# A list scheduler's due times taken backwards from TensorE's list, fewer and larger opening transfers, and spare matrix products in TensorE's idle stretches

## The chip, the cores and the metric

The kernel runs on one core of a Trainium2 chip. The metric is the device time of one execution in microseconds (us). The engines are TensorE (PE, with its weight loads as PEld), VectorE (DVE), ScalarE (ACT), GpSimd (POOL) and SyncE (SP), whose queue issues nearly all the transfers.

## The reference

Two operations, one on the other's result. First a light convolution: for each of 33280 tokens (8 batches of 4160) and each of 8 heads, a softmax over 7 taps weighs the last 7 tokens. Then a layer with a maximum of three projections:

```python
w = np.exp(weight_gen - weight_gen.max(-1, keepdims=True))
w = w / (w.sum(-1, keepdims=True) + 1e-09)
x_unf = x_pad[:, idx, :].reshape(B, S, K, H, group)      # 7 taps of 192 features
out = np.einsum('bshk,bskhg->bshg', w, x_unf).reshape(B * S, D)
h = np.maximum(np.maximum(out @ w1, out @ w2), out @ w3)  # 192 -> 768
return (h @ w_out).astype(np.float32)                     # 768 -> 192
```

x and weight_gen are float32; the four weight matrices are float64.

## The kernel before

**Tiles and stages.** Each of the 128 partitions holds 260 consecutive tokens. They are worked off in 65 chunks of four tokens per partition (512 tokens). `load_super` loads the first chunk alone and then two chunks at a time: `wt` (the tap weights) and `xt` (the tokens, and ahead of them six of the tokens before). The first two loads miss those six in the tile of a partition's predecessor, so halo rows are copied from the neighbouring partition's end: one transfer for each batch (line 305), in the first load half of them on ACT's queue. `softmax` has seven steps: maximum (DVE), subtraction (POOL), exponential (ACT), sum (DVE), addition of 1e-9 (DVE, line 344, tile `den`), reciprocal (DVE), product (POOL).

`taps` makes a chunk's convolution: for each of four tokens a product over seven taps on POOL (`r`, line 370) and its sum on DVE (`acc`, line 382). `blocks` turns the chunk so that features lie on partitions: for chunks 0 and 1 on TensorE (lines 402 and 403), for all later ones with one 32x32 block transpose on DVE (`room`, line 421) and 24 small copies on ACT (line 432). `parts` splits the result into high and low parts for fp32r products: `xa_hi`, `xa_lo`, `xb`, `xc`.

**Products.** All products of the main part stand at line 802, in `products`. Each bank (an accumulator of 128 x 512) is computed in two halves of 64 rows of the array, lower (list L) and upper (list U); between the lower half's last product and the upper half's first stands a nop in SP's queue (line 808). `up` makes for each of six j two banks of nine products, for w2 - w1 and w3 - w1; then ReLU on ACT (`m`, line 859), the maximum on DVE (line 867), and the split into `h_hi` (ACT, line 871) and `h_lo` (DVE or POOL, line 878). `down` makes for each of four tokens 18 products of each half, with w_out and with the composed matrix w1 @ w_out (`wca`, `wcb`), and adds on DVE (line 935). The order on TensorE is written out by hand: the twelve up-groups of a chunk, in whose middle (`DOWN_AT`) stand the four down-groups of the chunk before it.

**The opening.** The weights come as float64 and are converted by bit operations in `single`: one step on ACT (line 573) and four on DVE (lines 579 to 604), for nine tiles of the upper 128 rows (`prepare_a`, whose products are `wa_hi` and, on POOL, `wa_lo`, line 643), three tiles of the lower 64 rows (`prepare_b`: `wb_hi`, `wb_lo`) and three of w_out (`prepare_down`). After chunk 0's up-groups TensorE turns w1 (`turn_weights`, lines 731 and 733) and after half of chunk 1's it composes w1 @ w_out (`compose`, line 750; `wca` and `wcb`, lines 759 and 767).

**The order of the work.** Every operation is a task with an engine, a cost, the tasks it depends on, the buffers it holds and a due time. `Plan.order` simulates the engines: whenever one is free, it starts among its ready tasks whose buffers are to be had the one with the smallest due time. TensorE's lists L and U alone are worked off in their written order. The order of starts in this simulation is the order of the program on each engine. Due times come from fixed offsets to `needed(c)`, 22 + 21 c us, in most places, and from a running clock behind the products:

```python
    def needed(c):
        return FIRST + PERIOD * c
...
            p = plan.add(
                "POOL", 2.75, product, [ready[s], *loads[s][1]], due - 26 + 3 * t, [hr, hx, hw]
            )
```

Of the kernel before, what the change touches and what calls it, by code (L numbers as in the profile page):

```python
# [20 lines left out]
class Hold:  # L21


    def __init__(self, pool):
        self.pool, self.users, self.taken, self.tile = pool, 0, False, None


class Task:
    def __init__(self, engine, cost, emit, deps, due, holds, end):
        self.engine, self.cost, self.emit, self.due = engine, cost, emit, due  # L30
        self.holds, self.after = holds, []
        self.end = cost if end is None else end
        self.missing = 0
        for d in deps:
            d.after.append(self)
            self.missing += 1
        for h in holds:
            h.users += 1


class Plan:
# [4 lines left out]
    LATENCY = 0.12  # L46

    def __init__(self, pools):
        self.free = dict(pools)
        self.waiting = {"L": [], "U": []}  # L50
        self.tasks = []

    def add(self, engine, cost, emit, deps=(), due=0.0, holds=(), end=None):
# [3 lines left out]
        if engine in self.FIXED:  # L57
            self.waiting[engine].append(t)
        return t

    def order(self):
        ready, busy, events, done = {}, {}, [], []
        at = dict.fromkeys(self.FIXED, 0)
        for t in self.tasks:
            ready.setdefault(t.engine, [])
            busy.setdefault(t.engine, 0.0)
            if t.missing == 0 and t.engine not in self.FIXED:
                heapq.heappush(ready[t.engine], (t.due, t.n, t))

        def can(t):  # L70
            need = {}
            for h in t.holds:
                if not h.taken:
                    need[h.pool] = need.get(h.pool, 0) + 1
            return all(self.free[p] >= n for p, n in need.items())

        def start(t, now):
            for h in t.holds:
                if not h.taken:
                    h.taken = True  # L80
                    self.free[h.pool] -= 1
# [3 lines left out]
            heapq.heappush(events, (now + t.cost, 0, t.n, t, "free"))  # L85
            heapq.heappush(events, (now + t.end, 1, t.n, t, "given"))
            heapq.heappush(events, (now + t.end + self.LATENCY, 2, t.n, t, "seen"))

        now = 0.0
        while True:  # L90
            for e in ready:
                if busy[e] > now + 1e-9:
                    continue
                if e in self.FIXED:
                    k = at[e]
                    if k < len(self.waiting[e]):
                        t = self.waiting[e][k]
# [16 lines left out]
            while events and events[0][0] <= now + 1e-9:  # L114
                _, _, _, t, what = heapq.heappop(events)
                if what == "given":
                    for h in t.holds:
                        h.users -= 1
                        if h.users == 0:
                            self.free[h.pool] += 1  # L120
                elif what == "seen":
                    for a in t.after:
                        a.missing -= 1
                        if a.missing == 0 and a.engine not in self.FIXED:
                            heapq.heappush(ready[a.engine], (a.due, a.n, a))
        assert len(done) == len(self.tasks), (len(done), len(self.tasks))
        return done


@with_exitstack  # L130
def lightconv_maxout_kernel(
# [30 lines left out]
    DOWN_AT = 3  # L162
    ON_POOL = (1, 4)
# [19 lines left out]
    ident = const.tile([P, P], F32, name="ident")  # L183
    wa_hi = const.tile([P, NJ, NI, P], F32R, name="wa_hi")
# [47 lines left out]
    plan = Plan(counts | {"conv": 3})  # L232
# [24 lines left out]
    PERIOD = 21.0  # L257
    FIRST = 22.0

    def needed(c):  # L260
        return FIRST + PERIOD * c

# [3 lines left out]
    def transfer(cost, emit, deps=(), due=0.0, holds=(), on="SP"):  # L266
        issue = plan.add(on, 0.45, emit, deps, due, holds)
        return plan.add("DMA", cost, lambda: None, [issue], due, holds, end=cost + 2.0)
# [4 lines left out]
    def load_super(s):  # L273
# [3 lines left out]
        due = needed(cs[0]) - 40  # L277

# [10 lines left out]
        w = transfer(0.0005 * n * H * K, weights, (), due, [hw])  # L289
        if a >= PAD:  # L290
            t = [transfer(0.0005 * (n + PAD) * D, tokens, (), due + 0.1, [hx])]
        else:
            z = PAD - a
            zero = plan.add(
                "DVE", 1.1, lambda: pin(nc.vector.memset(buf(hx)[:, :z], 0.0)), (), due, [hx]
            )
            t = [transfer(0.0005 * (n + a) * D, tokens, (), due + 0.1, [hx])]
            for b in range(B):
                on = "ACT" if s == 0 and b % 2 else "SP"

                def rows(b=b, on=on):
                    to = slice(b * PB + 1, (b + 1) * PB)
                    q = nc.scalar if on == "ACT" else nc.sync
                    pin(
                        q.dma_start(
                            out=buf(hx)[to, :z], in_=xf[to.start - 1 : to.stop - 1, NT - z :]
                        )
                    )

                t.append(transfer(0.1, rows, [zero], due + 0.2, [hx], on))  # L310
# [5 lines left out]
    def softmax(s):  # L316
        n = len(supers[s]) * TC
        due = needed(supers[s][0]) - 32
# [8 lines left out]
            [loads[s][0]], due, [hr, hw],  # L327
# [4 lines left out]
            [a], due + 1, [hr, hw],  # L332
# [3 lines left out]
            [b], due + 2, [hw],  # L336
# [4 lines left out]
            [c], due + 3, [hd, hw],  # L341
        )
        e = plan.add(
            "DVE", 0.3, lambda: pin(nc.vector.tensor_scalar_add(part(hd), part(hd), 1e-9)),  # L344
            [d], due + 3, [hd],
        )
        f = plan.add(
            "DVE", 0.6, lambda: pin(nc.vector.reciprocal(part(hd), part(hd))), [e], due + 3, [hd]
# [4 lines left out]
            [f], due + 4, [hd, hw],  # L353
# [5 lines left out]
    def taps(c):  # L359
# [3 lines left out]
        due = needed(c)  # L363
        sums = []
        for t in range(TC):
            hr = hold("r")

            def product(t=t, hr=hr):
                pin(
# [11 lines left out]
            def total(t=t, hr=hr):  # L381
                pin(nc.vector.tensor_reduce(buf(ha)[:, t], buf(hr), axis=AX.X, op=ALU.add))  # L382
# [4 lines left out]
            sums.append(plan.add("DVE", 1.55, total, [p], due - 22 + 3 * t, [hr, ha]))  # L387
        return ha, sums

    def blocks(c, ha, sums, wait):  # L390


        due = needed(c)
        if c < ON_TENSOR:
            ba, bb = hold("bank"), hold("bank")
            got = []
            for t in range(TC):
# [7 lines left out]
                got.append(plan.add("L", 0.6, turn, [sums[t], *wait], due, [ba, bb, ha], end=0.9))  # L405
# [4 lines left out]
        def places():  # L410
# [10 lines left out]
            "DVE", 0.97, lambda: pin(nc.vector.transpose(places()[2], buf(ha))), sums, due - 12,  # L421
# [3 lines left out]
        for q, f in enumerate(range(0, D, 32)):  # L425
            for p in range(0, P, 32):

                def move(f=f, p=p):
# [3 lines left out]
                    pin(nc.scalar.copy(to[:, :, p : p + 32], b[p : p + 32, :, f : f + 32]))  # L432

                got.append(plan.add("ACT", 0.296, move, [turned], due - 11 + q, [hv]))
        return [hv], lambda: places()[:2], got

    def parts(c, hs, places, got):
        due = needed(c)
# [5 lines left out]
            "ACT", act(CH), lambda: pin(nc.scalar.copy(buf(ah), places()[0])), of_a, due - 3,  # L444
# [5 lines left out]
                due - 2.5, [k, *hs],  # L450
# [7 lines left out]
        def a_low():  # L458
            pin(
# [3 lines left out]
        def b_low():  # L463
            pin(
# [5 lines left out]
        lo = plan.add(name, cost, a_low, [hi], due - 1.5, [al, ah, *hs])  # L470
        bl = plan.add(name, cost, b_low, cs, due - 1.4, [b, k, *hs])
# [35 lines left out]
    w_due = lambda jp, i: FIRST + 4 * jp + 2 * i  # L507

    a_in, b_in, d_in = {}, {}, {}

    def load_a(jp):
        for i, w in enumerate(words[:3]):
# [8 lines left out]
                (), w_due(jp, 0) - 22, [a_hold(jp)],  # L521
            )

    def load_b(jps):
        got = []
        for i, w in enumerate(words[:3]):
            for odd, h in enumerate(halves):
                got.append(
                    transfer(
                        0.3 * len(jps),  # L530
                        lambda i=i, w=w, odd=odd, h=h: pin(
                            nc.sync.dma_start(  # L532
                                out=raw_b()[h, jps[0] : jps[-1] + 1, i].rearrange(
                                    "p j n w -> p j (n w)"
                                ),
                                in_=w[P:].rearrange("p (j o n) -> p j o n", j=NP, o=2)[
# [495 lines left out]
```

## Time and profile before

| what | value |
|---|---|
| median of 3 runs | 1441.08 us (1439.87 to 1443.25) |
| the profiled execution's own time | 1444.6 us |
| its span, first to last instruction | 1442.8 us |
| mean granted clock of TensorE | 0.987 |
| TensorE busy | 1402.0 us (97%) |
| DVE, ACT, POOL busy | 1043.4, 1117.3 and 1104.2 us (72%, 77%, 77%) |

How to read the profile: a row of a group names the line, the engine, the operation, the tile written and those read, their shapes, the count, the busy time and the mean of one in ns, and then the idle time of the engine ahead of it with the instruction that ended it. A row of the chain of waits has a start, a length and what the program's end waited for in that time; SPq is SP's queue. A row of a stretch has the stretch, its length, each engine's busy time with the number of its instructions, the granted clock of TensorE as a share, the DMA engines' busy share and GB/s. TensorE's clock has no record ahead of 39.9 us in this trace, and the rows show 1.00 there; the products at that time lie 0.43 us apart, as in the rows at 0.50.

### The profile page before, as it was taken

How to read it: one execution, taken by the hardware profiler on the slowest of the kernel's cores; microseconds unless marked ns; L12 is line 12 of the kernel's file. 1: busy time of each engine (PE TensorE's matmuls, PEld its weight loads, DVE VectorE, ACT ScalarE, POOL GpSimd, SP SyncE). 2: the span in 40 equal slices, each digit the busy share in tenths (PEclk: the TensorE clock that was granted, in tenths of full speed). 3: DMA queues.
4: the chain of work that ended last, by engine and by line, in shares of the span. 5: the costliest groups of instructions: out<-in, count | busy, mean ns of one | idle time of the engine just before them, and what ended most of it. 6: DMA issues, size and time to landing. Idle time of an engine off the chain costs nothing.

```text
span 1442.8 us, 37119 instructions
## 1 busy us (share of the span) xinstructions
PE 1402.0 (97%) x14878; PEld 1366.1 (95%) x14878; DVE 1043.4 (72%) x1433; ACT 1117.3 (77%) x2828; POOL 1104.2 (77%) x609
## 2 busy tenths in 40 slices
PE   2889999999999999999999999999999999999999
PEld 1579999999999999999999999999999999999998
DVE  7867777777777787777778777877877677777543
ACT  3547878878877887787788778877888887788773
POOL 6769888778877887887788778778877877787421
PEclk9679999999999999999999999999999999999999
DMA  7102111111111111111011111101111111110000
GB/s 249 46 1 79 57 68 57 68 68 57 68 46 46 57 68 68 68 57 64 28 57 68 68 68 57 68 25 67 57 68 68 57 68 44 48 57 24 23 21 26
DMA packets 23405, 85.08 MB, mean 59 GB/s; under 512 B 2768, under 2 KB 9544, under 8 KB 19136
## 3 DMA queue, kind: packets, MB, share of 16 engines
q1 hardware_dynamic: 23112, 82.44, 15.5%
q8 instruction: 116, 1.90, 0.5%
q14 instruction: 57, 0.47, 0.1%
q10 hardware_dynamic: 120, 0.28, 0.1%
HBM read 57.15 MB, written 25.56 MB: 57 GB/s over the span
## 4 chain that ended last, share of the span: by engine, by line
PE 95%; POOL 1%; DMA 1%; ACT 1%; SPq 1%; DVE 1%; issue 0%; POOLq 0%
PE bank L802 95%; POOL r L370 1%; DMA xt<-in_x_dram 1%; SPq L532 1%; DVE den L344 0%; ACT room L432 0%; DMA raw<-in_moe_w_dram 0%; SPq L516 0%; PE bank L733 0%; ACT m L859 0%; POOL wa_lo L643 0%; PE bank L731 0%; ACT wb_hi L684 0%; DVE acc L382 0%; ACT bank L573 0%
## 5 line engine op out<-in xcount | busy, mean ns | idle before, releaser
L370 POOL TENSOR_TENSOR r<-xt,wt 128x1344 f32<-128x1344 f32 x260 | 727.1, 2845 | 143.2 <-DVE acc L382 142.9
L802 PE MATMUL bank<-wo,h_hi 64*128 64x384 f32 x3120 | 675.0, 357 | 0.0
L802 PE MATMUL bank<-wo,h_lo 64*128 64x192 f32 x3120 | 603.4, 249 | 0.0
L432 ACT COPY room<-room 32x128 f32<-32x128 f32 x1512 | 448.4, 297 | 79.0 <-DVE room L421 55.9
L802 PEld LDWEIGHTS bank<-wo,h_lo 64*128 64x128 f32 x3120 | 493.0, 188 | 0.0
L802 PEld LDWEIGHTS bank<-wo,h_hi 64*128 64x128 f32 x3120 | 489.2, 186 | 0.0
L802 PE MATMUL bank<-xa_hi,wa_hi 64*128 64x512 f32 x1560 | 479.9, 394 | 6.0 <-ACT wa_hi L637 3.4
L802 PE MATMUL bank<-xa_hi,wa_lo 64*128 64x512 f32 x1560 | 477.9, 390 | 3.4 <-POOL wa_lo L643 3.3
L802 PE MATMUL bank<-xa_lo,wa_hi 64*128 64x512 f32 x1560 | 476.8, 391 | 0.5 <-DVE xa_lo L460 0.5
L382 DVE TENSOR_REDUCE acc<-r 128x192 f32<-128x1344 f32 x260 | 399.8, 1538 | 0.6 <-POOL r L370 0.3
L859 ACT ACTIVATE m<-bank 128x512 f32<-128x512 f32 x390 | 234.5, 601 | 71.4 <-PE bank L802 66.7
L935 DVE TENSOR_TENSOR o<-bank,ob 128x192 f32<-128x192 f32 x260 | 92.4, 356 | 268.7 <-ACT ob L928 268.5
L802 PE MATMUL bank<-xb,wb_hi 64*128 64x512 f32 x780 | 284.5, 390 | 0.3 <-DVE xb L465 0.3
L802 PE MATMUL bank<-xc,wb_hi 64*128 64x512 f32 x780 | 281.1, 390 | 0.2 <-ACT wb_hi L684 0.2
L802 PEld LDWEIGHTS bank<-xa_hi,wa_hi 64*128 64x128 f32 x1560 | 255.3, 186 | 13.5 <-ACT wa_hi L637 4.3
L802 PEld LDWEIGHTS bank<-xa_hi,wa_lo 64*128 64x128 f32 x1560 | 255.3, 186 | 11.2 <-POOL wa_lo L643 5.6
L802 PEld LDWEIGHTS bank<-xa_lo,wa_hi 64*128 64x128 f32 x1560 | 254.9, 187 | 6.4 <-DVE xa_lo L460 1.5
L802 PE MATMUL bank<-xc,wb_lo 64*128 64x512 f32 x780 | 258.0, 389 | 0.0
L867 DVE TENSOR_TENSOR bank<-bank,m 128x512 f32<-128x512 f32 x260 | 179.0, 689 | 42.2 <-PE bank L802 24.3
L878 POOL TENSOR_TENSOR h_lo<-m,h_hi 128x512 fp32r<-128x512 f32 x130 | 171.7, 1321 | 40.0 <-ACT h_hi L871 39.9
L802 PE MATMUL bank<-wca,xa_hi 64*128 64x384 f32 x520 | 183.4, 353 | 0.0
L878 DVE TENSOR_TENSOR h_lo<-bank,h_hi 128x512 fp32r<-128x512 f32 x260 | 172.4, 681 | 11.4 <-ACT h_hi L871 11.2
(79 smaller groups left out, 2012.5 us busy)
## 6 DMA issues: line engine op xcount, KB each, us to landing
xt<-in_x_dram SPq DMA_DIRECT2D x31, 1344.0 KB, 5.8
out_dram<-o SPq DMA_DIRECT2D x64, 384.0 KB, 2.3
wt<-in_weight_gen_dram SPq DMA_DIRECT2D x32, 224.0 KB, 2.6
h_hi<-in_moe_w_dram SPq DMA_DIRECT2D x6, 256.0 KB, 2.9
xt<-in_x_dram SPq DMA_DIRECT2D x1, 1152.0 KB, 5.8
h_lo<-in_moe_w_dram SPq DMA_DIRECT2D x6, 128.0 KB, 4.0
raw<-in_moe_w_dram SPq DMA_DIRECT2D x3, 256.0 KB, 3.6
room<-in_moe_w_out_dram SPq DMA_DIRECT2D x2, 384.0 KB, 6.4
```

Source lines behind the costliest of these rows:

```text
L370: nc.gpsimd.tensor_tensor(buf(hr).rearrange("p (h g) k -> p k h g", g=G), buf(hx)[:, la + t : la + t + K].rearrange("p k (h g) -> p k h g" ...
L382: pin(nc.vector.tensor_reduce(buf(ha)[:, t], buf(hr), axis=AX.X, op=ALU.add))
L432: pin(nc.scalar.copy(to[:, :, p : p + 32], b[p : p + 32, :, f : f + 32]))
L532: nc.sync.dma_start(out=raw_b()[h, jps[0] : jps[-1] + 1, i].rearrange("p j n w -> p j (n w)"), in_=w[P:].rearrange("p (j o n) -> p j o n", ...
L802: ins = nc.tensor.matmul(buf(hb)[:, :n], w()[h], v()[h], start=half == 0 and first, stop=half == 1 and last,)
L859: lambda: pin(nc.scalar.activation(buf(hm), buf(hb), AF.Relu)), [made], due,
L867: lambda: pin(nc.vector.tensor_tensor(buf(keep), buf(hb), buf(hm), op=ALU.max)),
L878: eng.tensor_tensor(buf(hl)[:, j], buf(keep), buf(hh)[:, j].bitcast(F32), op=ALU.subtract)
L935: nc.vector.tensor_tensor(buf(ho)[:, t], buf(hb)[:, :D], buf(hq), op=ALU.add)
```

## The change

**Due times.** `needed` and the offsets go. Most tasks have no due time of their own any more. Products get the time at which TensorE would come to them if it never waited, from the running clock; what follows a product keeps its due time behind that clock. `start_by` then goes backwards through all tasks: each must start so early that the earliest of those that depend on it can start in time. The costs in the plan are smaller (a tap 2.6 for 2.75, one of the 24 small copies 0.207 for 0.296, other ACT and DVE operations by about 0.1), with a lag behind each; transfers hold one of eight places (`flight`) in the plan.

**Transfers.** The halo rows come with four strided transfers on SP for each of the two loads, in place of eight on SP and ACT. The lower rows of the weights come in six transfers for all three pairs, in place of six for the first and six for the other two.

**Addition.** The 1e-9 of the softmax is added on ACT.

**Spare products.** A tile `spare` (four copies of the identity, written by ACT at the start) is multiplied with itself into a bank that nothing reads. The plan is made once; in every stretch over 0.6 us of its first 100 in which neither list L nor U has a product running, groups of products are put into list L, one group for each 2 us, with as many as fill 0.7 of it. Each group waits for the last task of DVE, POOL or ACT that ends ahead of it in the plan. Then the plan is made again with them.

```diff
+    def start_by(self):
+        for t in reversed(self.tasks):
+            latest = [a.by - self.LATENCY - t.end for a in t.after]
+            if t.due is not None:
+                latest.append(t.due)
+            t.by = min(latest, default=1e6)
...
-                heapq.heappush(ready[t.engine], (t.due, t.n, t))
+                heapq.heappush(ready[t.engine], (t.by, t.n, t))
...
+    def put(self, k, engine, cost, emit, deps, holds):
+        t = self.add(engine, cost, emit, deps, None, holds)
+        self.fixed[engine].insert(k, self.fixed[engine].pop())
+        return t
+
+    def idle(self, until):
+        found, end = [], 0.0
+        for t in sorted((t for e in self.FIXED for t in self.fixed[e]), key=lambda t: t.start):
+            if t.start > until:
+                break
+            if t.start > end:
+                found.append((end, t.start))
+            end = max(end, t.start + t.cost)
+        return found
+
+    def before_time(self, time):
+        for k, t in enumerate(self.fixed["L"]):
+            if t.start >= time - 1e-9:
+                return k
+        return len(self.fixed["L"])
...
+    SHARE = 0.7
+    UNTIL = 100
+    PACE = ("DVE", "POOL", "ACT")
...
     def vec(n):
-        return 0.15 + 0.00105 * n
+        return 0.062 + 0.00104 * n
     def act(n):
-        return 0.18 + 0.00084 * n
+        return 0.08 + 0.00083 * n
     def gps(n):
-        return 0.1 + 0.0024 * n
+        return 0.12 + 0.0022 * n
...
-            for b in range(B):
-                on = "ACT" if s == 0 and b % 2 else "SP"
...
+            step = 2
+            while step <= PB:
+                def rows(step=step):
+                    to = buf(hx)[step // 2 :: step, :z]
+                    of = xf[step // 2 - 1 :: step, NT - z :][: P // step]
+                    pin(nc.sync.dma_start(out=to, in_=of))
+                t.append(transfer(0.38 * z / step, rows, [zero], None, [hx]))
+                step *= 2
...
-            "DVE", 0.3, lambda: pin(nc.vector.tensor_scalar_add(part(hd), part(hd), 1e-9)),
-            [d], due + 3, [hd],
+            "ACT", 0.25,
+            lambda: pin(nc.scalar.activation(part(hd), part(hd), AF.Copy, bias=1e-9)),
+            [d], None, [hd],
...
-                "POOL", 2.75, product, [ready[s], *loads[s][1]], due - 26 + 3 * t, [hr, hx, hw]
+                "POOL", 2.6, product, [ready[s], *loads[s][1]], None, [hr, hx, hw]
...
-                got.append(plan.add("ACT", 0.296, move, [turned], due - 11 + q, [hv]))
+                got.append(plan.add("ACT", 0.207, move, [turned], None, [hv]))
...
                 t = plan.add(
-                    "LU"[half], slot, emit, [*deps, *(before if first else [])], 0,
+                    "LU"[half], slot, emit, [*deps, *(before if first else [])], at,
                     [hb, *holds], end=end,
                 )
+                at += slot
...
     load_a(0)
-    load_b([0])
+    load_b()
     load_a(1)
-    load_b([1, 2])
     load_a(2)
...
+    spots = []
+    ends = sorted(
+        (t.start + t.end, t.n, t) for t in plan.order() if t.engine in PACE and t is not made
+    )
+    for a, b in plan.idle(UNTIL):
+        k = plan.before_time(b)
+        while b - a > 0.6:
+            span = min(b - a, 2.0)
+            past = [t for e, _, t in ends if e <= a]
+            spots.append((k, int(SHARE * span / 0.2275 + 0.5), past[-1:]))
+            a += span
+    hf = hold("bank")
+    for k, n, deps in reversed(spots):
+        def fill(n=n, deps=deps):
+            for q in range(n):
+                ins = pin(nc.tensor.matmul(buf(hf), spare[:, :P], spare, start=True, stop=True))
+                if q == 0:
+                    for d in deps:
+                        after(ins, d.ins)
+        plan.put(k, "L", 0.2275 * n, fill, [made_spare, *deps], [hf])
     for t in plan.order():
-        t.emit()
+        t.ins = t.emit()
```

More of the change, by code (lines that the diff above doesn't have):

```diff
@@ L45, with add @@
     FIXED = ("L", "U")
-    LATENCY = 0.12
+    LATENCY = 0.1
+    LAG = {"DVE": 0.09, "ACT": 0.1, "POOL": 0.05}
     def __init__(self, pools):
-        self.free = dict(pools)
-        self.waiting = {"L": [], "U": []}
+        self.pools = dict(pools)
+        self.fixed = {"L": [], "U": []}
         self.tasks = []
-    def add(self, engine, cost, emit, deps=(), due=0.0, holds=(), end=None):
+    def add(self, engine, cost, emit, deps=(), due=None, holds=(), end=None):
+        end = cost + self.LAG.get(engine, 0.0) if end is None else end
         t = Task(engine, cost, emit, list(deps), due, list(holds), end)
@@ L72, in can @@
             for h in t.holds:
-                if not h.taken:
+                if h not in taken:
                     need[h.pool] = need.get(h.pool, 0) + 1
-            return all(self.free[p] >= n for p, n in need.items())
+            return all(free[p] >= n for p, n in need.items())
         def start(t, now):
             for h in t.holds:
-                if not h.taken:
-                    h.taken = True
-                    self.free[h.pool] -= 1
+                if h not in taken:
+                    taken.add(h)
+                    free[h.pool] -= 1
             t.start = now
@@ L247, in vec, with transfer @@
     def vec(n):
[L248 removed]
+        return 0.062 + 0.00104 * n
     def act(n):
[L251 removed]
+        return 0.08 + 0.00083 * n
     def gps(n):
[L254 to L257 removed]
+        return 0.12 + 0.0022 * n
     FIRST = 22.0
[L260 to L261 removed]
+    clock = [FIRST]
     queue = {"SP": 0.0}
[L266 to L268 removed]
+    def transfer(cost, emit, deps=(), due=None, holds=(), on="SP"):
+        held = [*holds, hold("flight")]
+        issue = plan.add(on, 0.45, emit, deps, due, held)
+        return plan.add("DMA", cost, lambda: None, [issue], due, held, end=cost + 1.8)
     loads = {}
@@ L403, in turn @@
                     pin(nc.tensor.transpose(buf(bb)[:DB, to], acc[:, t, P:], ident))
-                got.append(plan.add("L", 0.6, turn, [sums[t], *wait], due, [ba, bb, ha], end=0.9))
+                got.append(plan.add("L", 0.6, turn, [sums[t], *wait], clock[0], [ba, bb, ha], end=0.9))
             return [ba, bb], lambda: (buf(ba), buf(bb)[:DB]), got
@@ L420, in blocks @@
         turned = plan.add(
-            "DVE", 0.97, lambda: pin(nc.vector.transpose(places()[2], buf(ha))), sums, due - 12,
+            "DVE", 0.86, lambda: pin(nc.vector.transpose(places()[2], buf(ha))), sums, None,
             [hv, ha],
@@ L424, in blocks @@
         got = []
-        for q, f in enumerate(range(0, D, 32)):
+        for f in range(0, D, 32):
             for p in range(0, P, 32):
@@ L443, in parts @@
         hi = plan.add(
-            "ACT", act(CH), lambda: pin(nc.scalar.copy(buf(ah), places()[0])), of_a, due - 3,
+            "ACT", act(CH), lambda: pin(nc.scalar.copy(buf(ah), places()[0])), of_a, None,
             [ah, *hs],
@@ L733, in turn @@
                 pin(nc.tensor.transpose(b[:, to : to + DB], b32[h, jp, 0], ident[h, h]))
-        got = plan.add("L", 0.5, turn, [one_a[jp], one_b[jp], made, *u_last()], 0, [hb], end=0.8)
+        got = plan.add("L", 0.5, turn, [one_a[jp], one_b[jp], made, *u_last()], clock[0], [hb], end=0.8)
         turned_w[j] = plan.add(
@@ L754, in mult @@
                     )
-            got = plan.add("L", 2.4, mult, deps + u_last(), 0, [hb, hw1t], end=2.8)
+            got = plan.add("L", 2.4, mult, deps + u_last(), clock[0], [hb, hw1t], end=2.8)
             hi = plan.add(
@@ L787, in after @@
             mybir.DependencyInfo(mybir.DependencyClass.Sync, mybir.DependencyReason.DATA),
-            reason="the two halves of the rows don't write to a bank together",
+            reason="an order that no data gives",
         )
@@ L792, in products @@
     def products(hb, terms_of):
-        begun, before = {}, []
+        begun, before, at = {}, [], clock[0]
         for half in range(2):
@@ L951, in down @@
             )
-    made = plan.add("POOL", 1.0, lambda: make_identity(nc, ident), (), -50)
+    made = plan.add("POOL", 1.0, lambda: make_identity(nc, ident), (), 0)
+    made_spare = plan.add(
+        "ACT", act(CH),
+        lambda: pin(
+            nc.scalar.copy(
+                spare.rearrange("p (t n) -> p t n", n=P),
+                ident.unsqueeze(1).broadcast_to([P, TC, P]),
+            )
+        ),
+        [made], 0,
+    )
     for s in range(len(supers)):
```

203 lines of the change are left out of this document (94 added, 109 removed).

## The prediction

> **What bounds the kernel now.** I read the page first, then the products by stretch, then the opening piece by piece, then the chain of waits. From the page (busy shares; 40 slices in tenths; granted clock of TensorE):
>
> ```profile
> span 1442.8 us, 37119 instructions
> PE 1402.0 (97%) x14878; PEld 1366.1 (95%) x14878; DVE 1043.4 (72%) x1433; ACT 1117.3 (77%) x2828; POOL 1104.2 (77%) x609
> PE   2889999999999999999999999999999999999999
> PEclk9679999999999999999999999999999999999999
> ```
>
> TensorE is full from the fourth slice on; only the first three slices (108 us) have idle time and a low clock. How much they lose shows in the products of line 802 by stretch (stretch, length, busy and count on PE and on the weight loads, clock, DMA):
>
> ```profile
> 0.00:160.00 160.00, 110.34 (x844) 96.02 (x846) 0.88 0.28 95
> 160.00:1400.00 1240.00, 1240.00 (x13550) 1223.29 (x13548) 1.00 0.15 55
> 1400.00:1442.80 42.80, 39.44 (x434) 38.31 (x432) 1.00 0.08 29
> ```
>
> In the middle 13550 products take 1240 us, 10.93 a microsecond. The first 160 us hold 844 of them, 77 us of work at that rate, so about 80 us are lost there; the last 42.8 us hold 434, so 3 us are lost at the end. The change can win only in the opening. It can lose anywhere. Piece by piece the opening is this (the same columns with DVE, ACT and POOL behind PE and PEld):
>
> ```profile
> 0.00:26.33 26.33, 2.76 (x8) 0.95 (x9) 16.63 (x32) 6.53 (x15) 15.55 (x17) 1.00 0.72 215
> 26.33:64.88 38.55, 30.72 (x108) 21.55 (x108) 31.95 (x59) 18.96 (x42) 35.58 (x28) 0.78 0.26 93
> 64.88:70.88 6.00, 5.54 (x27) 3.64 (x26) 5.82 (x8) 3.18 (x9) 2.21 (x3) 0.70 0.56 226
> 70.88:82.37 11.49, 11.16 (x54) 8.80 (x55) 5.92 (x10) 9.63 (x27) 6.66 (x4) 0.71 0.00 1
> 82.37:92.22 9.85, 4.63 (x28) 4.17 (x27) 8.71 (x9) 3.46 (x10) 9.50 (x5) 0.94 0.01 2
> 92.22:101.36 9.14, 9.14 (x53) 9.14 (x55) 3.27 (x3) 0.00 (x0) 5.22 (x2) 0.50 0.00 0
> 101.36:112.20 10.84, 10.84 (x121) 10.80 (x122) 7.46 (x10) 4.66 (x11) 5.10 (x3) 1.00 0.10 38
> ```
>
> These are: before the first product; the twelve up-groups of chunk 0; turning w1 and chunk 1; six up-groups of chunk 1; composing and the stall in the first down-group; down-groups of chunk 0, cold; the same, warm. Next the chain of waits (start, length, what):
>
> ```profile
> 47.19 2.65 POOL r L370
> ...
> 51.68 2.67 POOL r L370
> ...
> 54.93 2.60 POOL r L370
> 57.53 0.62 POOL wa_lo L643
> ...
> 58.20 6.75 PE bank L802 x23
> ...
> 86.42 1.46 DVE acc L382
> 87.88 4.04 DVE den L344
> 91.92 0.26 DVE wcb L767
> ```
>
> Two wrong orders stand here. Three taps, which later chunks need, ran on GpSimd ahead of the last `wa_lo` that chunk 0 waited for; and a sum and a softmax addition ran on VectorE ahead of the `wcb` that the first down-group waited for.
>
> **The change part by part.** *First product, at 26.33.* From the order in time (start, length, engine, line):
>
> ```profile
> 9.01 10.23 POOL L370 TENSOR_TENSOR r<-xt,wt 128x1344 f32<-128x1344 f32 x4
> ...
> 14.99 1.54 DVE L382 TENSOR_REDUCE acc<-r 128x192 f32<-128x1344 f32 x1
> ...
> 23.82 0.47 PE L402 MATMUL bank<-ident,acc 128*128 128x128 f32 x1 [2.03 <-DVE acc L382]
> ...
> 25.70 0.57 ACT L444 CAST xa_hi<-bank 128x512 fp32r<-128x512 f32 x1
> ```
>
> The taps end at 19.24; with the sum straight behind (1.54), the two turns (0.47 the first, some 0.9 both) and `xa_hi` (0.57) the product could start at 22.3. Gain 4.
>
> *Merged transfers.* SP's and ACT's issues in the opening:
>
> ```profile
> 2.10 3.11 ACTq L305 DMA_DIRECT2D xt<-in_x_dram  x4
> 2.13 4.76 SPq L305 DMA_DIRECT2D xt<-in_x_dram  x4
> 7.84 3.75 SPq L532 DMA_DIRECT2D h_lo<-in_moe_w_dram  x6
> 12.81 5.55 SPq L305 DMA_DIRECT2D xt<-in_x_dram  x8
> 19.79 3.91 SPq L532 DMA_DIRECT2D h_lo<-in_moe_w_dram  x6
> ```
>
> The halo rows go from 4 issues on ACT and 12 on SP to 8 on SP; the lower rows of the weights from 12 issues to 6, each as large as the two before. SP spent 17.97 us on its 24 and will spend at the same mean (5.55/8 and 3.91/6) 8 x 0.69 plus 6 x 0.65, or 9.4; everything behind, the weights of the third pair above all, is issued some 8.6 us earlier. ACT comes free 3.1 us earlier for the exponential. Against it, the first lower weights now come with three pairs: the two old batches took 3.8 us each, so they may be up to 4 us later. I book no gain beyond the 4 above, whose end is set by GpSimd's four taps; if the weights were 4 us late, that 4 is gone. One more copy on ACT (`spare`) stands where ACT was idle; on the path it would cost about 0.6.
>
> *Chunk 0's up-groups, 38.55.* Off the chain go the taps (2.65 + 2.67 + 2.60 = 7.9), and half of the 6.75 of cold products, 3.4; together 11.3. But VectorE is busy 31.95 of the 38.55. Of this, three conversions of w_out (four operations each: 12 x 0.55 is 6.6 at most; neighbours overlap, I take 5.5) have late deadlines and move out:
>
> ```profile
> 55.21 0.55 DVE L595 SCALAR_TENSOR_TENSOR bank<-room,bank 128x384 uint32<-128x384 uint32 x1
> ```
>
> So VectorE needs 26.4, and behind its last conversion come about 2.5 of GpSimd, ACT and products: 29 at the least, a gain of 9.6 at most. An engine that is fed by four others is not full; I take 8. *Turning w1 and chunk 1, 6.00.* Half clock from 67.23: gain between 0 and 1.6, I take 1.
>
> *Clock.* TensorE in the stretches between its changes of clock:
>
> ```profile
> 39.92:43.33 3.41, 2.46 (x14) 1.00 0.00 0
> 43.33:50.16 6.83, 6.74 (x30) 0.50 0.00 1
> 50.16:53.57 3.41, 2.41 (x12) 1.00 0.02 5
> ...
> 63.81:67.23 3.42, 3.42 (x18) 1.00 0.99 363
> 67.23:77.47 10.24, 9.46 (x33) 0.50 0.09 36
> 77.47:91.12 13.65, 9.53 (x63) 1.00 0.01 2
> ```
>
> The clock changes on a grid of 3.41 us, up behind a stretch that was full, down behind stretches busy 2.46, 2.41 and even 3.42 of 3.41. So the spare products' share of 0.7 of idle time is near the edge, not safely over it. *Six up-groups, 11.49:* cold until 77.47, 6.6 us at half: gain 3.3 if warm, 0 if not; I take 3. *Stall, 9.85:* `wcb` needs no more than `wca` and the second composed bank, so the 1.46 and 4.04 go: gain 5. The addition itself moves from VectorE to ACT (one more on ACT for each of 33 loads; ACT is 77% busy, and 33 x 0.25 is 8 us if nothing covered it, but ACT idles in every chunk). *Down-groups, 9.14 cold:* they were cold because TensorE had just idled 5.2; without the stall they take half: gain 4.5, nearly certain.
>
> The Trainium skill, "TensorE: Matmul & The Clock Gate", section "Part 1: The HAM clock gate", says that the clock falls after at least one idle window of about 3.4 us. The trace agrees with the grid and not with "idle": it fell behind a window 72% busy (2.46 of 3.41). By the page any spare product in each window would hold it and the first rival below would have no chance; by the rows it keeps one.
>
> *Spare products.* TensorE is idle 37 us up to 101.36 (101.36 less 63.95 busy), so at a share of 0.7 at most 26 us go to them, some 110 products at the plan's 0.2275, in 18 groups of six. No spare product is in the trace: by the plan's figure a group lasts 1.4 us, cold twice that. Each waits for another engine's instruction, and everything on TensorE stands behind it; if TensorE waits anyway, it costs 0, if TensorE is late, 1.4. Bounds 0 and 18 x 1.4 = 25. I take 2 to 3, two groups, because they follow engines that are themselves late when TensorE is. One of eight banks goes to them in the opening.
>
> *What is late next.* VectorE works 79.8 up to 112.20. Less the 4 of `den` and four sums made ahead (4 x 1.54), 70 must fit in the 87 that a gain of 25 leaves, of which the first piece alone had 9.7 idle (26.33 less 16.63): 70 of 77. I take 2 off for it.
>
> Sum: 4 + 8 + 1 + 3 + 5 + 4.5 = 25.5, less 2.5 and 2: **21 us**. The profiled execution took 1444.6 with a span of 1442.8, the median is 1441.08; 1441.1 - 21 = **1420**. Ends: with the bounds (9.6, 1.6, 3.3, nothing off) 28, plus about 3 for the weights' earlier arrival, 1410; with the clock not held and VectorE full, about 10, 1431, and some 5 for spares in the way, 1436.
>
> **Rivals.** *The clock does not hold.* For it: 3.42 busy of 3.42 and yet a fall at 67.23. Against: cold spare products fill the idle stretches whole and bring it up again. Then the 3 and the 1 go, and groups of 2.7 us in places for 2.0 cost 2 more: gain 15, 1426. Chance 0.18.
>
> *VectorE or GpSimd bound the opening.* For it: 31.95 of 38.55 and 35.58 of 38.55 busy. Against: a part of that is early work. Then chunk 0 gains 2 and chunk 2 comes late: gain 11, 1430. Chance 0.15.
>
> *Slower: SP.* Lines 280 and 370 in the steady part:
>
> ```profile
> SPq L280 <- POOL r L370: 13.8, 27, 0.5
> L370 POOL TENSOR_TENSOR r<-xt,wt 128x1344 f32<-128x1344 f32 x231 | 649.1, 2857 | 140.6 <-DVE acc L382 140.6
> ```
>
> SP waits up to 0.5 at each load for a tap, since the plan has taps faster than they are; behind it in SP's queue stand the nops without which the upper half's products do not start. The new plan says 2.6 where 2.86 is measured (the old one 2.75). If each of 31 loads then held TensorE by over 21/31 = 0.7 us, the gain would be gone; with 0.9 it is 28 us, 1448. Against: GpSimd is idle 140.6 us ahead of its taps, so lateness does not add up, and the wait should grow by 0.2 to 0.3. Chance 0.08. Spares nearly all in the way (25 us) have 0.03.
>
> *The order does not get better,* because deadlines ignore that four taps queue on one engine: gains of clock and `wcb` alone, offset by spares: no change, 1441. Chance 0.04.
>
> **How the numbers follow.** Forecast 0.52, with its own range 1411 to 1426. What a measurement can tell from no change is about 0.2%, 2.9 us. Faster: 0.52 + 0.18 + 0.15 = 0.85, and 0.01 from the SP case being small; same 0.04; slower 0.10. The range 1409 to 1436 leaves out the slower cases, the unchanged one and a little below.
>
> **What would show it.** Right: first product near 22 to 23; last `wa_lo` before 46; no wait of TensorE on `wcb`; clock 1.00 through the down-groups; 844 products reached about 21 us earlier; the stretch from 160 at 10.93 a microsecond as before. Wrong: TensorE waits in the steady part, SP waits of over 1 us on line 280, spare products on the chain of waits, or VectorE on it from 25 to 60.

## The result and the profile after

The changed kernel took 1514.94 us (median of four runs, 1512.67 to 1515.25) against 1442.16 of the kernel before beside it: a ratio of 1.0503, with an interval of 1.0484 to 1.0522. It is 73 us slower; the prediction was 1420. The profiled execution took 1512.67 us with a span of 1510.9. Two executions among the experiments below, one of 4128.67 us and one of the kernel before of 2531.08, were slow ones and stand in no median or interval.

The head of the page of the kernel after, with TensorE's busy share and granted clock in 40 slices:

```profile
span 1510.9 us, 37266 instructions
PE 1458.0 (96%) x14988; PEld 1381.9 (91%) x14988; DVE 1035.5 (69%) x1400; ACT 1126.6 (75%) x2862; POOL 1105.4 (73%) x609
PE   8999999999999999999999999999999999999999
PEclk9999999999999999999999999999999999999999
```

The opening is fuller than before (8 and 9 where 2, 8 and 9 stood), though the spare products count in it, and the slices behind it look as full as they did. They are not, as the products of line 824 (line 802 before) show by stretch (stretch, length, busy and count on PE and on the weight loads, clock, DMA):

```profile
0.00:160.00 160.00, 104.65 (x946) 94.85 (x948) 0.96 0.28 95
160.00:1400.00 1240.00, 1204.45 (x12688) 1151.55 (x12687) 0.99 0.15 54
1400.00:1510.90 110.90, 107.64 (x1194) 106.83 (x1190) 0.99 0.06 23
```

The first 160 us now hold 946 products where they held 844: 102 at 10.93 a microsecond are 9.3 us won. The next 1240 us hold 12688 where they held 13550: 862 fewer, or 78.9 us lost. The difference, 69.6, is the difference of the two spans but for 1.5. So the opening did gain, by half of what was forecast, and a stretch that the prediction held unchanged lost over eight times as much as that. What TensorE and SP waited for behind 160 us (us in total, times, longest), in the kernel after:

```profile
PE bank L824 <- ACT h_hi L893: 22.3, 27, 1.0
PE bank L824 <- DVE h_lo L900: 12.6, 30, 0.4
...
SPq L318 <- POOL r L404: 18.2, 27, 1.4
```

In the kernel before, this view has no row of PE at all, and 13.8 us for SP. The down-groups now wait in every second chunk for ScalarE's `h_hi` and then for VectorE's `h_lo`. One such place, first ScalarE, then TensorE, in order of time (start, length, engine, line, and the idle time ahead with what ended it):

```profile
500.28 2.15 ACT L465 COPY room<-room 32x128 f32<-32x128 f32 x7 [0.49 <-DVE room L454]
...
505.88 1.22 ACT L465 COPY room<-room 32x128 f32<-32x128 f32 x4
507.12 0.62 ACT L893 CAST h_hi<-m 128x512 fp32r<-128x512 f32 x1
507.65 0.29 ACT L465 COPY room<-room 32x128 f32<-32x128 f32 x1
507.85 0.58 ACT L881 ACTIVATE m<-bank 128x512 f32<-128x512 f32 x1
508.45 1.22 ACT L465 COPY room<-room 32x128 f32<-32x128 f32 x4
509.70 0.59 ACT L893 CAST h_hi<-bank 128x512 fp32r<-128x512 f32 x1
```

```profile
510.34 0.44 PE L824 MATMUL bank<-wo,h_hi 64*128 64x384 f32 x1 [0.82 <-ACT h_hi L893]
511.27 0.35 PE L824 MATMUL bank<-wo,h_lo 64*128 64x192 f32 x1 [0.43 <-DVE h_lo L900]
```

Twenty-two of the 24 small copies lie between 500.28 and 510.6, ahead of ReLUs and `h_hi` that the down-group needs. ScalarE does not rest here after the first copy. Seven copies take 2.15 us, one 0.30: 0.308 from start to start. The plan counts 0.207. On 24 copies that is 2.4 us in 21, and the plan, which starts whatever is due first, put them where by its figures they fitted exactly. The copies stand on the chain of waits as well (share of the chain between 160 and 1450 us by line; first the kernel before, then the one after):

```profile
by line: PE bank L802 99.2%; DVE o L935 0.0%; ACT ob L928 0.0%; issue 0.0%
```

```profile
by line: PE bank L824 83.3%; ACT room L465 4.0%; DVE acc L416 3.3%; ACT m L881 2.7%; ACT h_hi L893 1.7%; DVE bank L889 1.6%; DVE h_lo L900 1.4%; issue 0.7%; POOL xb L497 0.3%; POOL xa_lo L492 0.3%; POOL r L404 0.3%; DVE room L454 0.2%; POOL
```

Before, this chain is TensorE's products and nothing else; after, a sixth of it is others' work, the copies (`room`, line 465) first.

A short wait also costs clock. The three stretches of the 3.41 us grid around this place (PE alone):

```profile
508.15:511.56 3.41, 2.16 (x19) 1.00 0.00 0
511.56:514.97 3.41, 3.41 (x28) 0.50 0.02 5
514.97:518.38 3.41, 3.41 (x50) 1.00 0.00 0
```

Behind a stretch busy 2.16 of 3.41 the clock was half for one stretch. There are nine such between 160 and 1400 us, 15 us of loss. With 35.5 us of idle TensorE (1240 less 1204.45) this makes 51 of the 78.9. The other 28 lie in stretches that the view counts as busy: a product's row lasts 0.25 us or more while the next one starts 0.09 us behind it, so a row covers the start of the wait that follows. Counted from start to start, 59 gaps between successive products are over 0.40 us, 55 us in all beyond 0.09 each; the kernel before has none. With the clock's 15 us that is 70 of the 78.9.

### The profile page after: what moved, and what is told of

The parts are those of the page before. It is cut to its first block, busy times and chain, and to the rows that moved or that the text cites. A ratio compares the mean times of both kernels' runs of the same rounds, so it can differ in the third digit from the quotient of the medians.

```text
span 1510.9 us, 37266 instructions
## 1 busy us (share of the span) xinstructions
PE 1458.0 (96%) x14988; PEld 1381.9 (91%) x14988; DVE 1035.5 (69%) x1400; ACT 1126.6 (75%) x2862; POOL 1105.4 (73%) x609
## 4 chain that ended last, share of the span: by engine, by line
PE 78%; ACT 8%; DVE 6%; POOL 5%; issue 2%; DMA 1%; SPq 0%; POOLq 0%; DVEq 0%; ACTq 0%
PE bank L824 78%; ACT room L465 4%; POOL r L404 3%; DVE acc L416 3%; ACT m L881 2%; ACT h_hi L893 2%; DVE bank L889 1%; DVE h_lo L900 1%; DMA raw<-in_moe_w_dram 0%; POOL xb L497 0%; POOL xa_lo L492 0%; POOL h_lo L900 0%; DMA h_hi<-in_moe_w_dram 0%; DMA wt<-in_weight_gen_dram 0%; POOL wt L387 0%
## 5 line engine op out<-in xcount | busy, mean ns | idle before, releaser
L404 POOL TENSOR_TENSOR r<-xt,wt 128x1344 f32<-128x1344 f32 x260 | 712.6, 2829 | 125.3 <-DVE acc L416 122.5
L824 PE MATMUL bank<-wo,h_hi 64*128 64x384 f32 x3120 | 678.5, 361 | 22.4 <-ACT h_hi L893 22.3
L824 PE MATMUL bank<-xa_hi,wa_hi 64*128 64x512 f32 x1560 | 506.7, 393 | 0.9 <-ACT wa_hi L661 0.9
L824 PE MATMUL bank<-xa_lo,wa_hi 64*128 64x512 f32 x1560 | 504.9, 392 | 1.6 <-POOL xa_lo L492 1.6
L824 PE MATMUL bank<-xa_hi,wa_lo 64*128 64x512 f32 x1560 | 501.2, 390 | 0.1
L824 PE MATMUL bank<-xc,wb_hi 64*128 64x512 f32 x780 | 295.0, 388 | 0.0
L824 PEld LDWEIGHTS bank<-xa_lo,wa_hi 64*128 64x128 f32 x1560 | 263.8, 185 | 9.1 <-POOL xa_lo L492 2.3
L824 PEld LDWEIGHTS bank<-xa_hi,wa_lo 64*128 64x128 f32 x1560 | 264.0, 186 | 8.4 <-POOL wa_lo L667 1.4
L824 PEld LDWEIGHTS bank<-xa_hi,wa_hi 64*128 64x128 f32 x1560 | 261.9, 185 | 9.9 <-ACT wa_hi L661 2.0
L824 PE MATMUL bank<-xc,wb_lo 64*128 64x512 f32 x780 | 270.1, 387 | 0.0
L950 ACT COPY ob<-bank 128x192 f32<-128x192 f32 x260 | 82.2, 317 | 180.6 <-PE bank L824 178.6
```

The source lines that it names most:

```text
L404: nc.gpsimd.tensor_tensor(buf(hr).rearrange("p (h g) k -> p k h g", g=G), buf(hx)[:, la + t : la + t + K].rearrange("p k (h g) -> p k h g" ...
L824: ins = nc.tensor.matmul(buf(hb)[:, :n], w()[h], v()[h], start=half == 0 and first, stop=half == 1 and last,)
L950: "ACT", act(D), lambda: pin(nc.scalar.copy(buf(hq), buf(hb)[:, D : 2 * D])), [made],
```

## The experiments

All times are to be read beside 1440 to 1443 us of the kernel before, run with each. Where no interval is given, it is one run.

**The copy's price, in both kernels.**

```diff
-                got.append(plan.add("ACT", 0.207, move, [turned], None, [hv]))
+                got.append(plan.add("ACT", 0.308, move, [turned], None, [hv]))
```

> The changed kernel with one number of the plan put back: a copy of line 465 costs 0.308 us (the pitch of copy after copy in the changed trace) in place of 0.207. Theory A (the plan's cheap copies put 24 of them ahead of ReLUs and h_hi, and the down-groups wait): the 82 us lost between 120 and 1430 us in the changed kernel fall under 5, the opening keeps its gain of 12, so about 1430 us. Rival B (the other smaller costs and lags do it): still 1495 to 1515. Rival C (the backward due times themselves order ACT badly): still over 1480, with TensorE waiting for h_hi.

The other way round, in the kernel before (0.296 to 0.207, its fixed due times kept):

> The kernel before with one number changed: a copy costs 0.207 in the plan in place of 0.296, due times and all else as before. Theory A: copies run ahead of h_hi here too, TensorE waits for h_hi in the steady part, 1480 to 1520. Rival C (due times): no change, 1441, since the old due times keep the order.

The first took 1450.8 us, ratio 1.0058 (1.0041 to 1.0074): 64 of the 73 us are gone. The second took 1494.4, 52 more than before. So the figure does most of it with either way of setting due times, and rival C fell. But the first left 23 us lost in the steady part (13299 products up to 1400 us for 13550), where under 5 were expected, with another wait, VectorE's `h_lo` alone. The second has nearly the same row, not the wait for `h_hi` that was expected (one, 0.7 us); its copies are 6.9% of the chain of waits (us in total, times, longest; the first kernel, then the second):

```profile
PE bank L824 <- DVE h_lo L900: 12.6, 26, 0.6
```

```profile
PE bank L802 <- DVE h_lo L878: 20.2, 26, 1.0
```

**The other prices.** First all old prices but the copy's, then all old prices with the copy at 0.308:

```diff
-    LAG = {"DVE": 0.09, "ACT": 0.1, "POOL": 0.05}
+    LAG = {}
-        return 0.062 + 0.00104 * n      # vec; act, gps, tap, sum, transpose, latency likewise
+        return 0.15 + 0.00105 * n
```

> The changed kernel with the old costs of all but the copies (vec, act, gps, tap 2.75, sum 1.55, block transpose 0.97, latency 0.12, no lags); the copy stays at 0.207. Theory A: still slow, 1490 to 1520. Rival B: the steady loss goes, 1425 to 1435.

> The changed kernel with the old costs throughout and the copy at 0.308; due times, transfers and spare products are those of the change. Theory A: as with the copy's cost alone, 1425 to 1435, no more than 5 us from it. Rival B: clearly faster than the copy's cost alone. Rival C: over 1480.

They took 1482.15 and 1432.89 us. With the copy at 0.207 the other prices are worth 33 us (1514.94 to 1482.15, a little under theory A's range), with the copy at 0.308 18 us (1450.8 to 1432.89): theory A's "no more than 5 us" fell, and rival B's "clearly faster" came. In the second TensorE has no wait behind 160 us, its steady part is nearly that of before (13519 products up to 1400 us), and product 306, the last of the opening, comes at 97.6 us for 108.8. The old prices, taken together, were the margin that the order lived on.

**Which of them.** With the copy at 0.308, ScalarE's old prices, and in another kernel GpSimd's (tap 2.75, other operations 0.1 + 0.0024 n, no lag):

> Copy at 0.308 as in e1, and the other ACT costs put back too (0.18 + 0.00084 n, no lag on ACT). e1 still lost 22.5 us between 120 and 1430 us, e4 (all costs put back) 6. Theory A2 (the rest is ACT as well: a ReLU or a cast of 512 has a pitch of 0.60 to 0.63 in the trace, 0.505 in the plan): the steady loss falls under 8 us, 1430 to 1437. Rival B2 (the tap at 2.6 where 2.83 is measured): unchanged, 1447 to 1452.

> Copy at 0.308 as in e1, and GpSimd's costs put back (tap 2.75, 0.1 + 0.0024 n, no lag on POOL), ACT and DVE as in the change. Theory A2: unchanged, 1447 to 1452, TensorE still waits for h_lo. Rival B2: the steady loss falls under 8 us, 1430 to 1437, and SP's waits for taps at the loads fall from 2.0 us at the most to 0.5.

ScalarE's gave 1447.79, 3 us less; the theory that its operations were too cheap fell. GpSimd's gave 1427.64, without a wait in the steady part. GpSimd's in two, the tap's 2.75 alone and then the rest alone:

> e1 (1450.8 us) with the tap's cost alone put back to 2.75; other GpSimd costs as in the change. If the tap is the second cause: steady loss from 22.5 to under 5 us, 1426 to 1432. If the GpSimd operations of 512 (0.12 + 0.0022 n and the lag) are: 1445 to 1452.

> The changed kernel with the copy at 0.308 and GpSimd's operations at 0.1 + 0.0024 a column without the lag, the tap left at 2.6 (the complement of the run with the tap alone, 1445.9). Theory A (the price of GpSimd's 512-element operations, not the tap's, makes the wait for h_lo): 1427 to 1431 us, no wait of TensorE for VectorE's h_lo past 160 us, the loss there under 4 us. Theory B (neither price alone does it; the order that the plan happens to give decides, and only the two together gave a good one): 1440 to 1450, with some 25 waits for h_lo of 0.4 to 1.0 us and 15 to 22 us lost past 120 us.

The tap alone gave 1445.9 (25 waits for `h_lo`, 12.0 us), the rest alone 1429.66, ratio 0.9922 (0.9907 to 0.9936), with one wait. So it is what the plan charges for GpSimd's work beside the tap's 2.6. In the steady part that is the price of the operations of 512 columns (`h_lo`, `xa_lo`, `xb`), 1.246 in the new plan and 1.329 in the old, or the lag of 0.05, which the new plan has behind every GpSimd operation, the tap too; no run separates the two. VectorE in order of time at the same place, first with the tap's price, then with the other:

```profile
520.28 1.54 DVE L416 TENSOR_REDUCE acc<-r 128x192 f32<-128x1344 f32 x1
521.74 1.43 DVE L889 TENSOR_TENSOR bank<-bank,m 128x512 f32<-128x512 f32 x2
523.08 1.54 DVE L416 TENSOR_REDUCE acc<-r 128x192 f32<-128x1344 f32 x1
524.54 1.28 DVE L900 TENSOR_TENSOR h_lo<-bank,h_hi 128x512 fp32r<-128x512 f32 x2
```

```profile
520.08 1.54 DVE L416 TENSOR_REDUCE acc<-r 128x192 f32<-128x1344 f32 x1
521.54 0.68 DVE L900 TENSOR_TENSOR h_lo<-bank,h_hi 128x512 fp32r<-128x512 f32 x1
522.13 0.69 DVE L889 TENSOR_TENSOR bank<-bank,m 128x512 f32<-128x512 f32 x1
522.73 1.55 DVE L416 TENSOR_REDUCE acc<-r 128x192 f32<-128x1344 f32 x1
524.19 0.68 DVE L900 TENSOR_TENSOR h_lo<-bank,h_hi 128x512 fp32r<-128x512 f32 x1
```

Above, both `h_lo` stand behind both sums, and TensorE waits for them at 525.27; below, one `h_lo` is through before the second sum. The price that heals is not the truer one: in the trace with the tap's price alone, an operation behind `h_lo` starts 1.25 us after it, which is the new price, and taps follow each other at 2.66, between new and old. Why 0.03 to 0.08 us more per operation turn this order is not settled; I know only that it does.

**The tap's price in the kernel before** (2.75 to 2.6), for the prediction's slower rival:

> The kernel before with the tap at 2.6 in place of 2.75, all else as before. If an underpriced tap alone makes TensorE wait for h_lo, due times apart: a steady loss of 10 to 25 us, 1450 to 1467. If it does so only with the backward due times: 1438 to 1444.

It took 1440.95 us against 1440.1, with 14.6 us of SP's waits for taps, the longest 1.0. That price alone is harmless.

**The spares.** All old prices, copy 0.308, no spare products (`UNTIL = 0`):

> e4 (all costs put back, 1432.9 us) without the spare products. If they are worth the clock in the opening: the clock falls to 0.50 in several stretches up to 90 us and the time is 4 to 10 us longer, 1437 to 1443. If the opening is set by DVE and GpSimd alone: within 2 us of 1433, whatever the clock does.

1434.48, ratio 0.995 (0.9938 to 0.9961), against 1432.89 with them, ratio 0.9933 by one run. That is 1.6 us, or 2.5 by the ratios; the eight runs without them spread by 4 us, so one run doesn't tell this from nothing.

**The transfers.** The same kernel with the old halo and weight transfers:

> e4 with the old transfers: halo rows by batch on SP and ACT, lower weight rows in two batches. In the changed kernel the first product came at 28.4 us, in the kernel before at 26.3, though the first turn came at 12.8 in place of 16.6. If the merged weight transfers, which go ahead of the first upper weights, hold it back: the first product comes 2 to 4 us earlier than in e4 and the time is the same or up to 3 us shorter. If SP's and ACT's issue time is what counts: taps and first product come 3 to 5 us later and the time is 3 to 8 us longer.

1432.97, ratio 0.9947 (0.9931 to 0.9962). Chunk 0 turns later (17.7 us for 13.7) and its first product starts later (29.5 for 26.4), yet product 306 is at 96.7 for 97.6: no difference by the end that one run of the other kernel could tell. Neither expectation came whole: the first product came later, as issue time would have it, and the time stayed.

Then, on top of GpSimd's old prices and the copy at 0.308, the weights' lower rows in two batches again, and the first upper weights ahead of them (by a due time of 13.5 in the plan), with the halo merged (how `load_b` takes its pairs is not shown):

```diff
-                (), None, [a_hold(jp)],
+                (), 13.5 if jp == 0 else None, [a_hold(jp)],
...
-    load_b()
+    load_b([0])
     load_a(1)
+    load_b([1, 2])
```

> e6 (copy 0.308 and GpSimd's old costs, 1427.6 us) with the lower weight rows in two batches again and the first three upper weights issued ahead of them; halo rows stay merged. In e6 the first conversion waited until 13.0 us for the six merged transfers and the first product came at 27.9. If the merged weights hold the first product: first conversion near 8 us, first product at 23.5 to 26, time 1422 to 1426. If VectorE's work is the bound whatever arrives first: first product earlier, the twelve up-groups of chunk 0 end as before (54.7), time within 2 us of e6.

1424.07, ratio 0.9889 (0.9827 to 0.9951). It was run again for an interval, and without spare products on the same chip:

> The kernel of the run with the upper weights first once more, for an interval on its ratio. Theory A (two prices of the plan, the copy and GpSimd's, made the loss, and the change's opening is a gain once they are right and the first upper weights are not held back): 1424 us, ratio 0.989 with both ends under 0.992. Theory B (the time of two runs was luck, and the order gives no more than the version with all old costs): 1431 to 1433, ratio 0.994.

> The version with the upper weights first, without the spare products. Theory A (the spares are worth little, since the stretches that they fill are waits for data and the clock falls only for 3.41 us after each): 1425 to 1427 us, 1 to 3 above the version with them, with one or two more stretches at half clock in the first 100 us. Theory B (they keep the clock, as the prediction had it, whose up-groups and down-groups together were 7.5 us): 1430 to 1433 us. Theory C (they cost more than they bring): 1421 to 1423.

1425.57 with the spares (median of five), ratio 0.9893 (0.9876 to 0.991), and 1428.64 without (of six), ratio 0.9916 (0.9902 to 0.993), between theories A and B. This version beats both kernels: 16 us under before, 89 under after. Its products by stretch, and three pieces of its opening (from product 109 to 162, to 163, to 306; DVE, ACT and POOL behind PE and PEld):

```profile
0.00:160.00 160.00, 111.63 (x1048) 102.29 (x1050) 0.98 0.29 97
160.00:1400.00 1240.00, 1240.00 (x13528) 1204.26 (x13527) 1.00 0.15 55
```

```profile
61.90:71.50 9.60, 8.80 (x57) 7.04 (x56) 8.45 (x11) 4.09 (x11) 5.12 (x3) 1.00 0.42 149
71.50:78.10 6.60, 5.58 (x30) 4.55 (x28) 2.13 (x5) 6.29 (x20) 2.20 (x2) 1.00 0.06 26
78.10:90.70 12.60, 12.60 (x144) 12.58 (x145) 6.99 (x10) 5.31 (x15) 10.23 (x5) 1.00 0.01 3
```

and the first and last of these pieces without spares:

```profile
61.70:74.20 12.50, 11.21 (x53) 8.95 (x54) 9.09 (x11) 4.97 (x12) 5.32 (x3) 0.73 0.35 128
...
78.60:96.50 17.90, 16.07 (x144) 15.79 (x145) 7.80 (x11) 7.33 (x22) 10.74 (x6) 0.81 0.01 1
```

In these pieces the spares keep the clock at 1.00 where it is 0.73 and 0.81 without them. By the medians that is 3.1 us, by the spread of the runs 1 to 6; the two executions shown lie 5.9 apart.

## Why the prediction was wrong, point by point

**The step that failed** is the one that is not there. The prediction says that the change "can lose anywhere" and then gives the steady part one price, under SP. The copy's 0.207 for 0.296, which stands in the list of changes, has no sentence; its effect on the steady part was put at nothing without a reason, and with the other prices it cost 78.9 us there. Its row was in the trace of before, and the mean is the same after:

```profile
L432 ACT COPY room<-room 32x128 f32<-32x128 f32 x1512 | 448.4, 297 | 79.0 <-DVE room L421 55.9
```

A mean of 297 ns beside a plan's 207, times 24 in a chunk of 21 us, on the engine that makes `h_hi`: enough for a rival of over 2 us a chunk. The prediction says of ScalarE only, for the addition, that it is 77% busy and idles in every chunk; an average says nothing of where its idle time lies. The Trainium skill, "Perfetto Trace Analysis", section "Optimizing Scalar/DVE Operations", says that a profiled latency on these engines is about twice the access overhead, since one half overlaps with the next instruction (some 93 ns on ScalarE). By that, as an estimate, 0.297 would mean a copy each 0.20 us, near the plan's figure. The traces show it where `h_hi` is followed by a ReLU (0.484 from start to start, at 0.589 long) and not where a copy follows a copy (0.308 at 0.297, the median of 1057 pairs); the measurement decides.

**The slower rival** had the sign and not the mechanism. SP's waits did grow, 13.8 to 18.2 us and 0.5 to 1.4 at the longest, but where nothing else was wrong (GpSimd's other prices old, the tap at 2.6) they were 10.0, again up to 1.4 at the longest, and TensorE waited once, for 0.5. And its 2.86 for a tap is a duration; in the kernel before, taps in a row start 2.67 apart, since each overlaps the next by 0.18. The plan was wrong by 0.07, not 0.26.

**The terms of the opening**, by pieces that end at the starts of products 1, 108, 109, 162 and 306 (us; the last two of the prediction's pieces are one here): the kernel before and after, and the last version, which has no steady loss. The rows of after stand below the table.

| term | predicted gain | before | after | gain | version | gain |
|---|---|---|---|---|---|---|
| first product, at | 4 | 26.3 | 28.4 | -2.1 | 22.0 | 4.3 |
| twelve up-groups of chunk 0 | 8 | 38.3 | 27.7 | 10.6 | 34.0 | 4.3 |
| turning w1, chunk 1 | 1 | 6.3 | 5.9 | 0.4 | 5.9 | 0.4 |
| six up-groups | 3 | 11.2 | 12.8 | -1.6 | 9.6 | 1.6 |
| stall and down-groups | 9.5 | 26.7 | 22.1 | 4.6 | 19.2 | 7.5 |
| sum, less 4.5 for spares and VectorE | 21 | | | 11.9 | | 18.1 |

```profile
0.00:28.40 28.40, 21.03 (x78) 14.34 (x78) 19.20 (x35) 12.02 (x27) 17.44 (x19) 1.00 0.95 313
28.40:56.10 27.70, 27.31 (x135) 20.65 (x135) 26.62 (x53) 13.59 (x32) 25.91 (x21) 0.94 0.01 5
56.10:62.00 5.90, 5.39 (x31) 3.32 (x29) 4.79 (x6) 4.40 (x12) 5.90 (x6) 1.00 0.00 0
62.00:74.80 12.80, 11.11 (x61) 8.65 (x60) 7.79 (x9) 6.54 (x20) 6.13 (x4) 0.87 0.36 125
74.80:83.70 8.90, 6.84 (x32) 5.30 (x30) 3.46 (x7) 6.09 (x18) 4.27 (x3) 0.88 0.01 3
83.70:96.90 13.20, 13.20 (x145) 13.19 (x146) 8.92 (x9) 3.04 (x7) 13.12 (x7) 0.95 0.00 1
```

*First product.* The prediction named the danger, lower weights that come with three pairs and "that 4 is gone", and booked it at nothing. It came worse: merged, they were issued ahead of the upper weights, and the first conversion of weights, at 6.89 before, waited until 12.65 (ScalarE's first conversion after, and in the version with the upper weights first):

```profile
12.65 1.39 ACT L599 ACTIVATE bank<-h_lo 128x384 f32<-128x384 f32 x3 [7.66 <-DMA h_lo<-in_moe_w_dram]
```

```profile
5.56 0.41 ACT L603 ACTIVATE bank<-h_hi 128x256 f32<-128x256 f32 x1 [0.60 <-DMA h_hi<-in_moe_w_dram]
```

There the product starts at 22.0, near the predicted 22.3; no run separates the order of these transfers from their split in two batches. But what came early is paid back in the up-groups: product 108 is at 56.1 and 56.0 in both, for a sum of 12 predicted and 8.5 and 8.6 measured. So 4 and 8 were not two gains to be added. The up-groups alone gained 10.6 after, over the prediction's bound of 9.6, and 4.3 in the version. VectorE is busy 26.62 of the 27.70 us after, close to the predicted 26.4, and GpSimd 25.91. The sign of `wa_lo` missed too: its last one ends at 51.6 (58.1 before, under 46 forecast), and taps still stand ahead of it on GpSimd. The rival that VectorE or GpSimd bound the opening, with its gain of 11, comes nearest to the 11.9; which of the two, no run tells.

*Six up-groups, stall, down-groups.* In the kernel after, ScalarE's copies for the next chunk stood ahead of `h_hi` here too: with their price alone mended, product 306 came at 92.0 for 96.9. `wcb` no longer ends the stall; the piece took 8.9 us all the same, and 6.6 in the version, since copies stand ahead of `wca` in both. In the kernel after, a group of five spare products, begun at 81.35 us, ran until 83.7 at half clock, and the first down-group began behind it at 83.68, though `wcb` was through at 82.4, 1.3 us earlier.

*Clock and spares.* The rival that the clock does not hold did not come: 0.87 to 1.00 in the rows above, where 0.78, 0.70, 0.71, 0.94 and 0.50 stood. 110 products were forecast, and 110 ran. They are in TensorE's way at places, as the sum's 2 to 3 us had it: beside that 1.3 us, three groups stand on the version's chain of waits, 3.4 us in all (start, length, what; line 1055 is the spare products):

```profile
23.73 1.58 PE bank L1055 x3
...
63.72 0.66 PE bank L1055 x2
...
76.99 1.19 PE bank L1055 x4
```

On balance they were worth about 3 us by the last pair of runs, not the better part of the 8.5 that the terms of clock (1, 3 and 4.5) add up to; without them the clock is down for part of the time only.

*What would show it wrong:* TensorE waiting in the steady part, and SP over 1 us at its loads, were named, and both came; a third, spare products on the chain of waits, came in the version. Of the signs of being right, the clock of 1.00 through the down-groups (0.95), the steady part and the first product at 22 to 23 failed in the kernel after.

## What to carry to other kernels

Where a planner writes the order of a tuned kernel, its prices are part of the kernel: check each changed one against the time from start to start of two such instructions in a row, not against a duration and not against another pair's, and multiply by the count in one period of the bound stage. An engine with a quarter of its time idle still fails a due time when a burst is packed by too low a price. And a price a little too high is a margin: before it is made exact, see what stands next behind it.

## What the runs showed of the hardware

- Small copies on ScalarE (32 x 128, SBUF to SBUF) start 0.308 us apart at a duration of 0.297, a gap of 0.012, while a ReLU behind `h_hi` starts 0.10 ahead of its end, and a tap on GpSimd 0.17 to 0.19 ahead of the end of the tap before. A copy doesn't overlap a ReLU beside it either: a ReLU behind a copy starts 0.32 us after it (median of 216 pairs). No run tells why.
- A wait of 0.8 and 0.4 us in one 3.41 us stretch is enough to halve the clock for the next (busy 2.16 of 3.41), nine times in 1240 us. All nine such stretches were busy 1.96 to 2.17 us; the next fullest, at 2.21 and 2.23, were followed by the full clock. In the opening of the kernel before the clock fell behind 2.46 too, so the busy time of these rows is not the whole measure. The Trainium skill, "TensorE: Matmul & The Clock Gate", section "Part 1: The HAM clock gate", has the clock fall after an idle window of that length; no stretch here was idle, so the trace does not agree.
- With the lower weight rows of all pairs asked for ahead of the upper ones, the DMA engines are 0.95 busy at 313 GB/s for 28.4 us, and the first conversion of weights still starts at 12.65 us. With the first upper weights ahead they are 0.78 busy at 245 GB/s for 22.0 us, and it starts at 5.56; the first use does not follow the rate.
